# Moving the chunk loads and the copies within the stacks from SyncE's DMA queue to ScalarE's, with two more chunk buffers

## Chip, cores and metric

The kernel runs on one core of one Trainium2 chip. The metric is the device time of one execution in microseconds (us); three runs were timed, and one further execution was profiled.

## The reference

Three layers follow each other, on a batch of 2 with 768 positions:

```
attention: 8 heads of 64; q, k, v
  bits   = (q @ proj > 0), 6 bits, the same for k; bucket = the number that the bits spell
  scores = q @ k.T / 8, and -1e9 where the buckets of q and k differ
  x      = softmax(scores) @ v, heads side by side: 768 x 512 per batch
layer 1:  u = x + real(fft over positions and features of x)
  un = layernorm(u);  x = u + relu(un @ w_ch1) @ w_ch2        (w_ch1 512 x 2048, w_ch2 2048 x 512)
layer 2:  theta = x @ w_theta;  zr, zi = x cos(theta), x sin(theta)
  u = x + w_tok_r @ zr + w_tok_i @ zi;  out = u + relu(u @ w_ch)
```

The weights arrive as float64 and are handed to the kernel as pairs of 32-bit words; everything else is float32.

## The kernel before

**Order of the work.** Batch 0's attention comes first, in an order written out by hand (`attention_first`, every engine's instructions kept in the order of the source). After it, batch 0's FFT, layer norm and MLP run beside batch 1's attention (`attention`), then batch 1's FFT and MLP beside layer 2's theta, and the token sums last. Behind the first part the order on each engine is set by a planner: it lays the instructions out by a simulated timeline and by the priorities that `at(us)` gives (a smaller number goes first). FFT of batch 0 has 50, the conversion of w1 60 to 72 for its first 12 chunks and 51 to 54 for the last four, w2 100 to 115, attention of batch 1 from 115 with a pace of 2.6 per score tile (its loads and stacks 60 earlier), the MLP of batch 0 from 170. Each engine then works through its own list in order.

**Float64 chunks.** `from_f64` (L169) takes the next buffer of `cvs` in turn, loads one chunk of 128 x 512 float64 (512 KB) into it (tile `r`), rebuilds float32 from the two words with two ACTIVATEs on ScalarE and one shift-and-or on VectorE, in place. `conv16` (L183) then splits the chunk into two float16 parts: the high one by an ACTIVATE (into `w1h`, `w2h`), the low one by a subtraction on GpSimd (into `w1l`, `w2l`), which is the last to read the buffer. There are three buffers (`NCV`), and `T["c2"]` of a second pool, 0 here. 16 chunks are w1, 16 are w2, all converted between batch 0's attention and the middle of batch 1's. The chunks of w_theta, the token weights and w_ch come later, through the same function. All loads are issued by SyncE (`T["lc"] = 's'`).

**Gates.** `after_gate` wraps instructions in `tc.issue_after(m)`, which orders an instruction behind `m` only if both belong to the same engine, DMA issues counted to the engine that issues them. The first 12 chunks stand in `after_gate("cv")`, whose two members are the ScalarE copy and the VectorE subtraction of the last half tile that batch 0's attention turns on TensorE (`turn_half`, L368).

**Stacks.** For batch 1, `prep` (L271) loads q, k and v of a pair of heads (`tt`, `vr`) on SyncE and builds one stack (`stk`, L301) per head, the operands of the score matmuls: ScalarE rounds q into rows 0 and k into rows 2, a DMA copies each of the two to the other half of the partitions (192 KB, two per head, 16 in all), GpSimd writes the remainders, and ScalarE the bucket rows.

**Scores to values.** A score tile goes TensorE (`pss`), VectorE (row maximum `nm`), ScalarE (exponential `p`), a split into two float16 parts on ScalarE or GpSimd and GpSimd, a DMA transpose issued by SyncE (`transposed`, L379; into tiles that the trace shows as `pt<-p`, `pt<-pt`, `x<-p`), and TensorE again (`pso`). The layer norm's output for the MLP goes through SyncE's DMA transposes too (`unT<-u`). The MLP's first matmuls are `psm<-unT,w1h`.

Of the kernel before, what the change touches and what calls it, by code (L numbers as in the profile page):

```python
# [13 lines left out]
U32 = mybir.dt.uint32  # L14
# [19 lines left out]
def f(t):  # L34
    return t.bitcast(F32)
# [35 lines left out]
def fused_kernel(ctx, tc, A, out):  # L71
    nc = tc.nc
    V, AC, PE, PL, SY = (Ordered(tc, e) for e in (nc.vector, nc.scalar, nc.tensor, nc.gpsimd, nc.sync))

    def pool(name, bufs=1, **kw):
        return tc.alloc_tile_pool(name=name, bufs=bufs, **kw)

    def mk(p, shape, dt, tag, **kw):
        return p.tile(shape, dt, tag=tag, name=tag, **kw)

    def mm(o, l, r, st, sp):
        PE.matmul(o, l, r, start=st, stop=sp)

    def pl_copy(out, in_, scale=1.0):
        PL.tensor_scalar(out=out, in0=in_, scalar1=scale, scalar2=0.0, op0=ALU.mult, op1=ALU.add)

    def stt(eng, out, in0, in1, op, scale=1.0):
        if eng is V:
            return V.scalar_tensor_tensor(out=out, in0=in0, scalar=scale, in1=in1, op0=ALU.mult, op1=op)
        assert scale == 1.0  # L90
        return eng.tensor_tensor(out=out, in0=in0, in1=in1, op=op)

    T = dict(
        pet='dpd', dup=1, c2=0, c0=46, cx=0, wm=6, gf=1, o2=0, xs=1, sb=2, al=[['p', 2], ['p2', 3], ['pt', 3]], cs='v', g0=1,
        lg=[[0, 2], [2, 4], [4, 6]], ub=2, pace0=1.6, lead=60, f0=50.0, w1=60.0, w1s=1.0, b1=115, pace1=2.6,
        w2=100.0, w2s=1.0, m0=170.0, f1=190.0, th=240.0, m1=290.0, z0=330.0, wt=300.0, n0=8, n1=16, k0=12, k1=16, c1=46, tp=16, i0=40, i1=[20, 10],
        ne=42, es=150, ld='ss', lc='s', ps=[[0, 3], [0, 5], [1, 0], [1, 5]])
    P3 = ((0, 0), (0, 1), (1, 0))

    const = pool("const")  # L100
# [14 lines left out]
    def PS(k):  # L115
        n = turn[k] % sum(c for _, c in ring[k])
        turn[k] += 1
        for p, c in ring[k]:
            if n < c:
                w = [128, 2, 512] if k == "s" else [128, 512]  # L120
                tag = "psm" if p in [x[0] for x in ring["m"]] else "ps" + k
                live[k] = p.tile(w, F32, tag=tag, name=tag)
                return live[k]
            n -= c
# [27 lines left out]
    def fill(n, k="o"):  # L152

        for _ in range(n):
            PE.matmul(live[k][:, 392:512], pat[:, 0], pat[:, 1, 0:120], start=True, stop=True)
# [13 lines left out]
    def from_f64(src, scale=1.0, n=CN):  # L169
        p = cvs[turn["cv"] % len(cvs)]  # L170
        turn["cv"] += 1
        r = mk(p, [128, 2 * CN], U32, "r64", bufs=NCV if p is cv_p else None)
        r = r[:, 0:2 * n]
        {"s": SY, "a": AC, "p": PL}[T["lc"]].dma_start(out=r, in_=src.bitcast(U32))
        lo, hi = r[:, 0:2 * n:2], r[:, 1:2 * n:2]

        AC.activation(out=lo, in_=lo, func=AF.Relu, scale=2.0 ** -29 * (1 - 2.0 ** -20), bias=c_half)

        AC.activation(out=f(hi), in_=f(hi), func=AF.Prelu, scale=scale * 2.0 ** -112, alpha=2.0 ** 32)
        V.scalar_tensor_tensor(out=lo, in0=hi, scalar=3, in1=lo, op0=ALU.logical_shift_left, op1=ALU.bitwise_or)  # L180
        return f(lo)

    def conv16(src, n, hi, lo, lo_eng):  # L183
        for i in range(n // CN):
            c = slice(CN * i, CN * i + CN)
            w = from_f64(src[:, c], 2.0)
            AC.activation(out=hi[:, c], in_=w, func=AF.Copy)
            stt(lo_eng(i), lo[:, c], w, hi[:, c], ALU.subtract)
            yield

    def conv32(src, n, hi, lo):
        for i in range(n // CN):
            c = slice(CN * i, CN * i + CN)
            w = from_f64(src[:, c])
            AC.activation(out=hi[:, c], in_=w, func=AF.Copy)
            stt(PL, lo[:, c], w, f(hi[:, c]), ALU.subtract)
            yield
# [13 lines left out]
        "p": one(kept[0], 0, 1) + one(kept[2], 2) + one(spare[0], 4) + one(spare[1], 4),  # L211
        "p2": one(kept[1], 0, 1) + one(spare[0], 0, 1), "pt": one(kept[2], 0, 1) + one(spare[0], 2, 3) + one(spare[1], 0, 1, 2, 3)}
    cvs = [cv_p] * NCV
    if T["c2"]:
        cv2_p = pool("cv2", T["c2"], side="right")
        cvs += [cv2_p] * T["c2"]
# [54 lines left out]
    def prep(b, j):  # L271

        tt = mk(at_p, [128, 2, S], F32, "tt")
        ld = {"s": SY, "a": AC, "p": PL}[T["ld"][b]]
        vr = mk(at_p, [128, 2 * NT * (D + 1)], F32, "vr")
        for o, i in ((tt[:, 0], A["qT"]), (tt[:, 1], A["kT"]), (vr, A["v"])):
            ld.dma_start(out=o, in_=i[b, j])
        pl_copy(tt[:, 1], tt[:, 1], 0.125)
        v2 = mk(vv_p, [128, 2, 2 * NT * (D + 1)], F16, "vv")

        def values():
            AC.activation(out=v2[:, 0], in_=vr, func=AF.Copy, scale=VS)
            stt(V, v2[:, 1], vr, v2[:, 0], ALU.subtract, VS)

        if j:
            values()
        yield
        st = []
        bits = mk(at_p, [64, 2, 384], BF16, "bits")
        ps = PS("s")  # L290
        into = [ps[:, g, 0:384] for g in range(2)]
        for g in range(2):
            for qk in range(2):
                mm(into[g][32 * qk:32 * qk + 32], projb, tt[:, qk, 384 * g:384 * g + 384], True, True)
        V.tensor_scalar(out=bits, in0=ps[0:64, :, 0:384], scalar1=0.0, scalar2=None, op0=ALU.is_gt)
        made[4 * b + j] = [st, v2.rearrange("p a (h k c) -> p a h k c", h=2, k=NT)]
        for h in range(2):
            yield
            dd, oo = half[h], half[1 - h]
            s = mk(st_p, [128, 4, S], F32R, "stk")  # L300
            st.append(s)  # L301
            AC.activation(out=s[dd, 0], in_=tt[dd, 0], func=AF.Copy)
            SY.dma_start(out=f(s[dd, 1]), in_=f(s[dd, 0]))
            stt(PL, s[oo, 1], tt[dd, 0], f(s[dd, 0]), ALU.subtract)
            AC.activation(out=s[dd, 2], in_=tt[dd, 1], func=AF.Copy)
            SY.dma_start(out=f(s[oo, 3]), in_=f(s[dd, 2]))
            stt(PL, s[dd, 3], tt[dd, 1], f(s[dd, 2]), ALU.subtract)
            pp = PS("s")
            for g in range(2):
                mm(pp[:, g, 0:384], pat[0:64, h], bits[:, g], True, True)  # L310
            if b and not j and not h:
                fill(T["i0"])
            for qk in range(2):
                i = half[h if qk else 1 - h]
                AC.activation(out=s[oo, 2 * qk].rearrange("p (a n) -> p a n", a=2), in_=pp[i, :, 0:384],
                              func=AF.Sign if qk else AF.Relu, bias=hb[i, qk:qk + 1])
            if not j and not h:
                values()
        yield
# [96 lines left out]
    def attention(b, t0, pace, lead, hi_eng, lo_eng, after=lambda b, j: None):  # L416
        x_t[b] = mk(x_p, [128, NT, DM], F32, "x")
        n, w = 0, soft["p2"][0].shape[1]
        for j in range(4):
            i = 4 * b + j  # L420
            if i not in made:
                at(t0 + pace * n - lead)
                with after_gate("p1" if b else None):
                    run(prep(b, j))
# [503 lines left out]
    h1, l1, c1, c2 = (ev(k) for k in ("aapap", "p", "p", "p"))  # L928
# [8 lines left out]
    al = [x for t in kept for x in one(t, *range(t.shape[1]))]  # L937
# [33 lines left out]
    def mlp(b, t0, gs):  # L971
        for g in gs:
            timed(mlp1(b, g, m_p, res, hs), t0 + 41 * g, 2.6)
            timed(mlp2(b, g, hs), t0 + 41 * g + 20, 2.6)

    mlp(0, T["m0"], range(3))
    del cvs[NCV:]
    for p in ([cv2_p] if T["c2"] else []) + [so_p, sm_p, st_p, vv_p, at_p]:
        p.release()
    ring.pop("o")[0][0].release()  # L980
# [44 lines left out]
    def conv_tok(half, n0=0, n1=2 * NT):  # L1025
        for n in range(n0, n1):
            w = from_f64(A["wtok"][half][:, TH * n:TH * n + TH], n=TH)
            hi, lo = (wt(k, n % 2, n // 2) for k in range(2))
            AC.activation(out=hi, in_=w, func=AF.Copy)
            stt(PL, lo, w, f(hi), ALU.subtract)  # L1030
            yield
# [153 lines left out]
```

## Time and profile before

| | us |
|---|---|
| median of 3 timed runs | 730.92 |
| lowest and highest | 729.13, 737.44 |
| the profiled execution | 728.28 |
| its span, first to last instruction | 726.5 |
| TensorE busy | 664.8 |
| VectorE, ScalarE, GpSimd busy | 402.6, 372.7, 370.1 |

The profiled execution's own time is 1.8 us longer than its span. PE is TensorE (PEld its weight loads), DVE VectorE, ACT ScalarE, POOL GpSimd, SP SyncE; SPq is SyncE's instruction queue, where DMAs are issued and issues wait for semaphores. Because every operation is recorded in a helper, nearly all rows carry line L62 or L64; the tile names tell them apart. A wait is put down to the instruction that came last. Issuing a DMA is not counted as busy time.

### The profile page before, as it was taken

The page shows a single profiled execution, that of the slowest core. Times are in us where ns is not written, and L with a number is a line of the kernel's source. Part 1 is how long each engine was busy: PE and PEld are TensorE (multiplying, and loading weights), DVE is VectorE, ACT ScalarE, POOL GpSimd, SP SyncE. Part 2 cuts the span into 40 slices and gives each one's busy share as a digit, 9 for nine tenths or more (in the row PEclk, how much of TensorE's full clock was granted, in tenths as well). Part 3 has the DMA queues.
Part 4 walks back from the last instruction along what each step waited for, and adds up shares of the span by engine and source line. Part 5 has one row for each costly group of instructions (what it writes and reads, how often), then busy time and mean ns, then how long its engine had stood idle before and what let it go on. Part 6 is the DMA issues. An engine that isn't in the chain of part 4 may idle for free.

```text
span 726.5 us, 13450 instructions
## 1 busy us (share of the span) xinstructions
PE 664.8 (92%) x5424; PEld 510.9 (70%) x5424; DVE 402.6 (55%) x655; ACT 372.7 (51%) x597; POOL 370.1 (51%) x312
## 2 busy tenths in 40 slices
PE   5798988669668898999999999999999899999998
PEld 2365556557557655786686786687485599999997
DVE  1566787865999665543377583255422476751222
ACT  2565565766988898773423152065325676730010
POOL 3787789586878888776660020033403446930000
PEclk9999999978699999999999999999999999999999
DMA  9896967459889999776560043011004631720202
GB/s 327 186 187 141 157 121 142 93 164 213 197 206 240 269 231 253 151 145 124 102 195 27 13 120 65 1 45 30 1 1 145 223 89 39 234 81 25 88 1 87
DMA packets 161469, 93.68 MB, mean 129 GB/s; under 512 B 137088, under 2 KB 147584, under 8 KB 161408
## 3 DMA queue, kind: packets, MB, share of 16 engines
q1 hardware_dynamic: 159472, 86.27, 51.3%
q0 software_dynamic: 1936, 6.57, 2.6%
q8 instruction: 42, 0.69, 0.4%
q14 instruction: 19, 0.16, 0.1%
HBM read 49.82 MB, written 6.29 MB: 77 GB/s over the span
## 4 chain that ended last, share of the span: by engine, by line
PE 48%; POOL 10%; issue 9%; DMA 6%; ACT 5%; DVE 4%; POOLq 0%; SPq 0%; DVEq 0%; ACTq 0%
PE psm L62 31%; PE psf L62 14%; POOL p L62 3%; ACT r L62 2%; PE pso L62 2%; POOL w1l L62 2%; DMA x<-p 2%; POOL stk L62 2%; PE pss L62 1%; DMA r<-in_wtok 1%; DMA r<-in_w 1%; POOL pt L62 1%; DVE r L62 1%; ACT stk L62 1%; POOL w2l L62 1%
## 5 line engine op out<-in xcount | busy, mean ns | idle before, releaser
L62 PE MATMUL psm<-unT,w1h 128*128 128x256 f16 x768 | 130.4, 274 | 0.1
L62 PE MATMUL psm<-unT,w1l 128*128 128x256 f16 x384 | 105.2, 274 | 0.0
L62 DVE SCALAR_TENSOR_TENSOR r<-r 128x512 uint32<-128x512 uint32 (+1 forms) x64 | 64.6, 1016 | 51.9 <-ACT r L62 49.2
L62 PEld LDWEIGHTS <-w1h 128*128 128x128 f16 (+1 forms) x774 | 75.1, 99 | 15.5 <-issue 4.5
L62 PEld LDWEIGHTS <-hh 128*128 128x128 f16 x384 | 37.1, 98 | 42.8 <-issue 2.2
L62 POOL TENSOR_TENSOR w1l<-r,w1h 128x384 fp32r<-128x384 f32 (+1 forms) x36 | 41.9, 1178 | 43.5 <-ACT w1h L62 43.5
L62 PE MATMUL pss<-stk 128*128 128x384 f32 x192 | 48.8, 384 | 15.2 <-ACT p L62 9.4
L64 PE MATMUL pss<-stk 64*128 64x384 f32 (+1 forms) x288 | 55.4, 470 | 6.4 <-ACT p L64 3.2
L62 DVE TENSOR_REDUCE nm<-pss 128x1 f32<-128x768 f32 x48 | 44.9, 949 | 29.0 <-PE pss L62 28.8
L62 PE MATMUL psm<-w2h,hl 128*128 128x512 f16 x192 | 60.3, 379 | 0.0
L62 PE MATMUL psm<-w2l,hh 128*128 128x512 f16 x192 | 59.8, 379 | 0.2 <-POOL w2l L62 0.2
L62 ACT ACTIVATE r<-r,chalf 128x512 uint32<-128x512 uint32 (+1 forms) x64 | 46.1, 720 | 26.2 <-DMA r<-in_wtok 10.2
L62 PE MATMUL psm<-w2h,hh 128*128 128x512 f16 x192 | 59.3, 379 | 0.0
L62 POOL TENSOR_TENSOR p<-p,p 128x768 f16<-128x768 f32 x32 | 54.7, 1715 | 6.6 <-ACT p L62 5.5
L62 ACT ACTIVATE p<-pss,nm 128x768 f32<-128x768 f32 x48 | 42.5, 892 | 28.1 <-DVE nm L62 23.3
L62 DVE SCALAR_TENSOR_TENSOR hl<-psm,hh 128x512 f16<-128x512 f32 x48 | 32.8, 687 | 41.9 <-ACT hh L62 41.8
L64 DVE TENSOR_REDUCE nm<-pss 128x1 f32<-128x768 f32 x48 | 43.6, 950 | 19.9 <-PE pss L64 19.8
L62 ACT ACTIVATE hh<-psm 128x512 f16<-128x512 f32 x48 | 28.2, 590 | 40.4 <-PE psm L62 40.4
L62 PEld LDWEIGHTS pss<-stk 128*128 128x128 f32 x192 | 34.6, 204 | 20.2 <-ACT p L62 11.9
L62 PEld LDWEIGHTS <-w1l 128*128 128x128 f16 x384 | 37.7, 98 | 5.7 <-issue 1.2
L62 ACT ACTIVATE r<-r 128x512 f32<-128x512 f32 (+1 forms) x64 | 39.5, 618 | 0.0
L62 POOL TENSOR_TENSOR stk<-tt,stk 64x768 fp32r<-64x768 f32 x16 | 31.1, 1945 | 11.5 <-issue 9.6
(322 smaller groups left out, 1552.2 us busy)
## 6 DMA issues: line engine op xcount, KB each, us to landing
r<-in_w SPq DMA_DIRECT2D x32, 512.0 KB, 4.5
r<-in_wtok SPq DMA_DIRECT2D x24, 384.0 KB, 3.8
vr<-in_v SPq DMA_DIRECT2D x8, 390.0 KB, 3.6
stk<-stk SPq DMA_DIRECT2D x16, 192.0 KB, 3.8
xT<-xs SPq DMA_DIRECT2D x12, 256.0 KB, 2.6
xt<-xT SPq DMA_DIRECT2D x4, 768.0 KB, 5.8
ct<-in_ct POOLq DMA_DIRECT2D x4, 579.0 KB, 7.3
sn<-in_sn POOLq DMA_DIRECT2D x4, 576.0 KB, 8.2
```

The lines of the kernel that those rows point to most:

```text
L62: return fn(*a, **k)
L64: self.last = fn(*a, **k)
```

## The change

Five buffers take the place of three for the chunks of w1 and w2 (`c2` goes from 0 to 2), the loads into them go to ScalarE's DMA queue (`loads = [AC]`), and so do the 16 copies within the stacks. Behind batch 1's attention and batch 0's MLP in the source, the list `loads` is set to SyncE and the two extra buffers are dropped, so that the later chunks are loaded as before.

```diff
     T = dict(
-        pet='dpd', dup=1, c2=0, c0=46, ...
+        pet='dpd', dup=1, c2=2, c0=46, ...
...
-        ne=42, es=150, ld='ss', lc='s', ps=[[0, 3], [0, 5], [1, 0], [1, 5]])
+        ne=42, es=150, ld='ss', ps=[[0, 3], [0, 5], [1, 0], [1, 5]])
...
         r = r[:, 0:2 * n]
-        {"s": SY, "a": AC, "p": PL}[T["lc"]].dma_start(out=r, in_=src.bitcast(U32))
+        loads[0].dma_start(out=r, in_=src.bitcast(U32))
...
     cvs = [cv_p] * NCV
+    loads = [AC]
     if T["c2"]:
         cv2_p = pool("cv2", T["c2"], side="right")
         cvs += [cv2_p] * T["c2"]
...
             AC.activation(out=s[dd, 0], in_=tt[dd, 0], func=AF.Copy)
-            SY.dma_start(out=f(s[dd, 1]), in_=f(s[dd, 0]))
+            AC.dma_start(out=f(s[dd, 1]), in_=f(s[dd, 0]))
             stt(PL, s[oo, 1], tt[dd, 0], f(s[dd, 0]), ALU.subtract)
             AC.activation(out=s[dd, 2], in_=tt[dd, 1], func=AF.Copy)
-            SY.dma_start(out=f(s[oo, 3]), in_=f(s[dd, 2]))
+            AC.dma_start(out=f(s[oo, 3]), in_=f(s[dd, 2]))
...
     mlp(0, T["m0"], range(3))
     del cvs[NCV:]
+    loads[0] = SY
```

## Rows read from the trace of the kernel before

**Rows 1.** Busy time by stretch: PE, PEld, DVE, ACT, POOL; PEclk, DMA share, GB/s.
```profile
137.00:211.00 74.00, 52.56 (x427) 43.26 (x426) 58.59 (x111) 58.19 (x92) 57.82 (x43) 0.79 0.76 185
211.00:320.00 109.00, 99.83 (x1004) 73.98 (x1001) 72.14 (x93) 90.27 (x131) 91.46 (x63) 0.98 1.02 221
...
436.00:726.00 290.00, 284.72 (x1704) 236.90 (x1701) 117.52 (x175) 109.95 (x202) 79.69 (x76) 1.00 0.24 72
```

**Rows 2.** TensorE's waits, 137 to 211 us: us in total, times, longest.
```profile
PE pss L62 <- ACT p L62: 11.3, 6, 3.4
PE pss L62 <- ACT stk L62: 5.5, 3, 3.2
```

**Rows 3.** TensorE's waits, 211 to 320 us.
```profile
PE pso L62 <- DMA x<-p: 3.6, 3, 1.9
PE pso L62 <- DMA pt<-pt: 2.7, 3, 1.7
PE pso L62 <- DMA pt<-p: 2.2, 2, 1.9
```

**Rows 4.** ScalarE's waits for chunks, 137 to 211 us, then 126 to 320 us.
```profile
ACT r L62 <- DMA r<-in_w: 6.5, 4, 3.4
...
ACT r L62 <- DMA r<-in_w: 8.7, 9, 3.4
```

**Rows 5.** Waits of SyncE's queue, 137 to 211 us, then 211 to 320 us.
```profile
SPq L62 <- POOL w1l L62: 30.5, 14, 6.7
...
SPq L62 <- POOL w2l L62: 13.6, 10, 2.8
```

**Rows 6.** Issues by tile, r and stk: ns shortest/median/longest, first and last start.
```profile
L62 SPq DMA_DIRECT2D r<-in_w x32: 327/384/1377, 8.1 to 276.6; - x32
...
L62 SPq DMA_DIRECT2D stk<-stk x16: 461/472/953, 134.6 to 318.3; - x16
```

**Rows 7.** Timeline of SyncE's queue, the first loads: start, us.
```profile
8.08 1.40 SPq L62 DMA_DIRECT2D r<-in_w  x3
```

**Rows 8.** Timeline of ScalarE: last copy of a turned half, first conversion.
```profile
133.38 0.49 ACT L64 ACTIVATE w1l<-psm 128x384 f16<-128x384 f32 x1 [0.56 <-PE psm L64]
...
137.70 0.76 ACT L62 ACTIVATE r<-r,chalf 128x512 uint32<-128x512 uint32 x1
```

**Rows 9.** Groups of ScalarE's instructions, 137 to 211 us: busy, mean ns | idle before.
```profile
L62 ACT ACTIVATE r<-r,chalf 128x512 uint32<-128x512 uint32 x16 | 12.2, 763 | 6.6 <-DMA r<-in_w 6.5
```

**Rows 10.** Chain of waits, 137 to 215 us: start, us, what.
```profile
198.47 4.09 DMA r<-in_w
```

**Rows 11.** Timeline of SyncE's queue, 205 to 245 us.
```profile
221.45 0.52 SPq L62 DMA_DIRECT2D r<-in_w  x1
222.08 1.43 SPq L62 DMA_TRANSPOSE x<-p  x1
...
237.40 1.20 SPq L62 DMA_DIRECT2D stk<-stk  x2
238.70 0.54 SPq L62 DMA_DIRECT2D r<-in_w  x1
239.28 2.20 SPq L62 DMA_TRANSPOSE x<-p  x1
```

**Rows 12.** Timeline of GpSimd, 221 to 246 us.
```profile
230.40 1.65 POOL L62 TENSOR_TENSOR p<-p,p 128x768 f16<-128x768 f32 x1
```

**Rows 13.** Timeline of TensorE, 198 to 320 us; in brackets the idle time before.
```profile
210.93 0.38 PE L62 MATMUL psm<-unT,w1h 128*128 128x256 f16 x2
...
229.38 0.73 PE L62 MATMUL pso<-vv,x 128*128 128x65 f16 x18 [1.93 <-DMA x<-p]
...
246.72 0.55 PE L62 MATMUL pso<-vv,x 128*128 128x65 f16 x12 [1.14 <-DMA x<-p]
```

**Rows 14.** DMA issues, 126 to 320 us, then 320 to 370 us: median us to landing.
```profile
pt<-p SPq DMA_TRANSPOSE x12, 5.0
...
pt<-p SPq DMA_TRANSPOSE x4, 3.8
```

More of the change, by code (lines that the diff above doesn't have):

```diff
@@ L93, in fused_kernel @@
     T = dict(
-        pet='dpd', dup=1, c2=0, c0=46, cx=0, wm=6, gf=1, o2=0, xs=1, sb=2, al=[['p', 2], ['p2', 3], ['pt', 3]], cs='v', g0=1,
+        pet='dpd', dup=1, c2=2, c0=46, cx=0, wm=6, gf=1, o2=0, xs=1, sb=2, al=[['p', 2], ['p2', 3], ['pt', 3]], cs='v', g0=1,
         lg=[[0, 2], [2, 4], [4, 6]], ub=2, pace0=1.6, lead=60, f0=50.0, w1=60.0, w1s=1.0, b1=115, pace1=2.6,
         w2=100.0, w2s=1.0, m0=170.0, f1=190.0, th=240.0, m1=290.0, z0=330.0, wt=300.0, n0=8, n1=16, k0=12, k1=16, c1=46, tp=16, i0=40, i1=[20, 10],
-        ne=42, es=150, ld='ss', lc='s', ps=[[0, 3], [0, 5], [1, 0], [1, 5]])
+        ne=42, es=150, ld='ss', ps=[[0, 3], [0, 5], [1, 0], [1, 5]])
     P3 = ((0, 0), (0, 1), (1, 0))
```

## The prediction

> **What bounds the kernel now.** I read the busy time by stretches first [rows 1]. From 436 us to the end TensorE is busy 284.72 of 290 us: it alone sets that time, and the change touches nothing there. The moved instructions stand where batch 1's attention runs beside batch 0's FFT and MLP, and there TensorE is short of work. I call 137 to 211 us stage A (TensorE busy 52.56 of 74 us) and 211 to 320 us stage B (99.83 of 109). The end follows from TensorE's idle time before 320 us, so each edit counts by what it adds to or takes from the 21.4 us idle in A and the 9.2 in B. Then I read whom TensorE waits for. In A it is ScalarE, for the exponentials and the stacks: 11.3 and 5.5 us [rows 2]. In B it is the DMA transposes: 3.6, 2.7 and 2.2 us, 8.5 in sum [rows 3]. Last come the queues on both sides of the change. ScalarE waits for a chunk 6.5 us in A and 8.7 from 126 to 320 us, so 2.2 outside A [rows 4]. SyncE's queue stands on GpSimd's release of a chunk buffer, 30.5 us in 14 waits in A and 13.6 in 10 in B [rows 5]; transposes stand behind those waits.
>
> So the change takes work from a queue that hurts TensorE in B and gives it to an engine that TensorE waits for in A. ScalarE is busy 58.19 of 74 us in A and 90.27 of 109 in B [rows 1].
>
> **What moves, and when.** 32 loads of w1 and w2 and 16 copies within the stacks, 48 issues [rows 6]. Three loads go out together from 8.08 us now [rows 7], because the gate on the first twelve chunks orders only instructions of the gating instructions' own engines, and those are ScalarE and VectorE (the two copies of the last turned half). Once the loads are ScalarE's own instructions, the same gate holds them behind ScalarE's copy at 133.38 us [rows 8]. So the early loads are lost, not gained: five go out from about 134 us. The first chunk is converted at 137.7 us [rows 8], so batch 0's attention keeps its time; I put 0 to 126 us at no change (1.5 MB less in its first 20 us, beside tables that it does not read).
>
> **The cost on ScalarE.** The trace has no DMA issued by ScalarE. The nearest rows are SyncE's: a load issue 0.38 us, a copy issue 0.47 (medians) [rows 6]. The least is nothing, if the issue goes by while an ACTIVATE still runs; the most I take is the longest copy issue, 0.95, for one that first has to see ScalarE's own result land. I take the medians, the nearest rows. Sixteen chunks are converted in A [rows 9]; with five buffers 21 loads are issued by its end, and 8 of the copies, so A gets 21 x 0.38 + 8 x 0.47 = 11.8 us (0 to 27.6), and B gets 11 x 0.38 + 8 x 0.47 = 7.9 (0 to 18.1). Queued behind each of these on ScalarE are the exponentials that TensorE waits for.
>
> **What ScalarE gets back.** With five buffers a chunk lies ready before its conversion comes up, so I take the waits for chunks as gone: -6.5 us in A, -2.2 in B (0 to these). Against that the first conversion waits for a load issued after 134 us and landing some 4.1 us later [rows 10]; other ScalarE work can stand in between, and I put 1 us (0 to 3). Net on ScalarE: A 11.8 - 6.5 + 1 = +6.3, B 7.9 - 2.2 = +5.7.
>
> How much of this reaches TensorE? In A, ScalarE has 15.8 us idle, 9.3 without the waits for chunks, and these take up a part; but TensorE's waits in A are mostly for ScalarE. I take half: +3.2. In B the MLP fills TensorE, and its longest waits are the three of [rows 3], none for ScalarE; I take a quarter: +1.4. At the medians the two lie between -6.5 (waits gone, issues hidden) and +12 (both nets in full). At 0.95 us for every issue, with nothing absorbed and nothing won, it would be 27.6 + 18.1 + 3 = +48.7; that end is far from the nearest rows.
>
> **What SyncE's queue gives back.** Two copies and a load hold SyncE from 237.40 us, and only at 239.28 comes a transpose [rows 11] whose operand GpSimd had ready at 232.05 [rows 12]. TensorE waits 1.14 us for it [rows 13]: with the 1.88 us of moved work away, all of that goes. The transpose at 222.08 has one moved load ahead of it (0.63 us from 221.45), of a wait of 1.93. That is 1.1 + 0.6 = 1.7 us. The rest of these waits is the transposes of the layer norm, which stay on SyncE, and the landing. In A SyncE's waits for GpSimd stand mostly where no transpose is ready. I take -1.7, from 0 to -8.5.
>
> The landing itself: transposes take 5.0 us to land between 126 and 320 us and 3.8 once the loads are over [rows 14]. The DMA engines are full in B (share 1.02) [rows 1] and the same bytes still pass them, so I count no quicker landing. The Trainium skill says the same in "DMA: Bandwidth & Descriptors" (section "Issuing engines are not separate DMA queues"): DMAs issued by several engines run on the same 16 DMA engines, and only the sequencer's issue time is saved. Its section "Queues, rings and completion order" there speaks for a gain, since each DMA engine takes turns between the rows of the two issuers, packet by packet, so that a transpose would no longer stand behind a whole load; by it the landing could fall toward 3.8 us. No row here has two such queues at once.
>
> **Sum.** +3.2 + 1.4 - 1.7 = +2.9 us. The profiled execution is 728.28 us, its span 726.5 and 1.8 around it; it becomes 731.2. The median of the runs shown is 730.92, 2.6 above the profiled one, so I forecast 734 for the median. The order on every engine is planned anew with the change; that has no row, and I leave room for it in the range.
>
> **Rivals.**
> 1. Slower: ScalarE becomes the bound of A, because a refill stands at the head of its queue until GpSimd has released the buffer. The planner puts a load where the buffer is just released, so more buffers do not loosen that wait; what SyncE now stands through at little cost, ScalarE would stand through with the exponentials behind it. For it: SyncE's 30.5 us over 14 waits in A [rows 5], and ScalarE 79% busy there. Against: part of those waits is only SyncE having nothing else to do. Price: the net 6.3 plus a fifth of 30.5 (6.1), 12.4 us. It decides once ScalarE loses more in A than its 9.3 us of other idle time: from there the first MLP matmul, at 210.93 us now [rows 13], starts later by the whole. 730.92 + 12.4 = 743. Chance 0.34.
> 2. Faster: the queue was the trouble. Transposes go out when ready and land without loads ahead: three quarters of the 8.5 us in B (-6.4); and the load in the chain of waits shortly before the first MLP matmul (198.47 us, 4.09 long) is gone [rows 10], with ScalarE's issues hidden under running ACTIVATEs: -10.5. 720. For it: both waits are there in the rows. Against: ScalarE's share, and the full DMA engines. Chance 0.27.
> 3. It does little that counts: both sides come out small, 726 to 736. With the forecast this holds 0.39.
>
> **How the numbers follow.** A measurement of this kernel tells about 1% (7.3 us) from no change. Within 1%: 0.39; faster by more: 0.27 (rival 2); slower by more: 0.34 (rival 1). The likeliest case alone runs from 725 to 738. The range reaches from 719, past rival 2, to 747, past rival 1; the far end of +48.7 stays in the two in ten left out.
>
> **What would show it.** Right: no load of a chunk before 133 us, then five; ScalarE's waits for chunks under 2 us in A; TensorE's waits for transposes in B near 7 us; its waits for ScalarE in A near 20. Wrong towards slower: ScalarE's queue standing before loads with GpSimd's w1l as releaser, first MLP matmul after 218 us. Wrong towards faster: first MLP matmul before 206 us, transposes landing in under 4.2 us, TensorE idle in A under 16 us. The argument as a whole is wrong if the time changes by over 1% with these rows unchanged.

## The result and the profile after

The changed kernel takes 744.49 us (median of 20 executions, 732.43 to 753.26), the kernel before 730.83 us on the same chips (20, 725.55 to 737.44). The ratio is 1.0143, with a 95% interval of 1.0110 to 1.0176: 1.4% slower, some 10.5 us. The ratio, here and below, compares fast executions alone: eleven of the changed kernel's twenty, over 1.5% above its quickest, are left out of it as slow, and over all twenty the medians lie 1.9% apart. The profiled execution of the changed kernel happens to be the quickest of its twenty (732.43 us, span 730.7), so the profile of a second execution of the same kernel, `e1_again` (span 739.3), is read beside it.

Busy time by stretch, the changed kernel; columns as in [rows 1]:

```profile
137.00:211.00 74.00, 49.30 (x397) 41.35 (x394) 65.74 (x98) 61.59 (x101) 58.29 (x44) 0.82 0.92 218
211.00:320.00 109.00, 102.12 (x1009) 76.18 (x1008) 71.30 (x103) 82.35 (x118) 85.29 (x59) 1.00 0.93 195
320.00:436.00 116.00, 110.72 (x970) 82.06 (x969) 67.18 (x146) 44.70 (x73) 46.99 (x44) 0.99 0.50 105
```

The same of `e1_again`:

```profile
137.00:211.00 74.00, 47.78 (x378) 39.73 (x377) 61.55 (x86) 56.86 (x93) 54.83 (x41) 0.81 0.85 206
211.00:320.00 109.00, 99.48 (x979) 74.10 (x977) 66.53 (x106) 82.03 (x120) 82.74 (x57) 0.95 0.91 192
```

In stage A TensorE is idle 24.7 us (74 less 49.30) in the quick execution and 26.2 in the second, against 21.4 before [rows 1]. Behind stage B, from 320 to 436 us, it is idle 5.3 us in the changed kernel, where before it was busy nearly all the time:

```profile
320.00:436.00 116.00, 115.77 (x982) 86.03 (x980) 68.17 (x148) 42.58 (x72) 44.04 (x42) 1.00 0.43 99
```

`e7_new_order_one_queue`, below, has 4.9 us there, so this part comes with the new order of the work. Over the whole span TensorE is idle 69.9 us in the quick execution (730.7 less 660.8 busy) and 69.8 in the second (739.3 less 669.5), against 61.7 before (726.5 less 664.8). So in both it stands idle some 8 us longer. What sets the two apart is TensorE's busy time for the same matmuls, at a mean granted clock of 0.977 and 0.958.

Whom TensorE waits for in stage A, the changed kernel, answering to [rows 2]:

```profile
PE pso L62 <- DMA pt<-pt: 7.0, 2, 6.1
PE pso L62 <- DVE x L62: 5.2, 1, 5.2
PE pss L62 <- ACT p L62: 3.6, 2, 2.8
...
PE pss L62 <- ACT stk L62: 1.2, 1, 1.2
```

The waits for ScalarE, 16.8 us before, are 4.8. What stands in their place is two waits for transposes (7.0 us, one of them 6.1) and VectorE (which `e7_new_order_one_queue`, below, waits for as long, 4.9 us). This is not what a ScalarE burdened with 48 issues would look like. Its queue shows why. Issues by tile, answering to [rows 6]:

```profile
L62 ACTq DMA_DIRECT2D r<-in_w x32: 329/334/1285, 131.5 to 249.7; - x32
...
L62 ACTq DMA_DIRECT2D stk<-stk x16: 468/484/1702, 132.7 to 322.2; - x16
```

And ScalarE's timeline, its engine (ACT) and its queue (ACTq) together:

```profile
131.44 0.49 ACT L64 ACTIVATE w1l<-psm 128x384 f16<-128x384 f32 x1 [0.56 <-PE psm L64]
131.46 0.39 ACTq L62 DMA_DIRECT2D r<-in_w  x1
...
156.10 0.49 ACT L62 ACTIVATE fa<-psm 128x386 fp32r<-128x386 f32 x1 [1.70 <-PE psm L62]
156.16 0.33 ACTq L62 DMA_DIRECT2D r<-in_w  x1
```

An issue of 0.33 us begins 0.06 us after an ACTIVATE of 0.49 us and is over before it: the queue issues while the engine works. (The first load, at 131.46, stands right behind the last copy of a turned half, as the gate demands.)

What did get worse is how long transfers take to land. DMA issues from 126 to 320 us with the median us to landing, the changed kernel, then `e7_new_order_one_queue`, which has nearly the same order of work with all DMAs on SyncE:

```profile
stk<-stk ACTq DMA_DIRECT2D x14, 192.0 KB, 6.3
...
tt<-in_kT SPq DMA_DIRECT2D x3, 384.0 KB, 7.0
pt<-p SPq DMA_TRANSPOSE x11, 3.9
pt<-pt SPq DMA_TRANSPOSE x11, 5.5
```

```profile
stk<-stk SPq DMA_DIRECT2D x14, 192.0 KB, 3.5
...
tt<-in_kT SPq DMA_DIRECT2D x3, 384.0 KB, 4.2
pt<-p SPq DMA_TRANSPOSE x11, 4.4
pt<-pt SPq DMA_TRANSPOSE x11, 4.9
```

The copies within the stacks nearly double, 3.5 to 6.3 us, and a load that stayed on SyncE's queue (`tt<-in_kT`) takes 7.0 in place of 4.2; one kind of transpose is quicker, another slower. A median hides the few transfers that matter, as the experiments show.

The first MLP matmul, at 210.93 us before [rows 13], on TensorE's timeline of the changed kernel, then of `e1_again`:

```profile
212.07 0.38 PE L62 MATMUL psm<-unT,w1h 128*128 128x256 f16 x2
```

```profile
217.84 0.38 PE L62 MATMUL psm<-unT,w1h 128*128 128x256 f16 x2
```

### The profile page after: what moved, and what is told of

It reads as the page before. It is cut to its first block, busy times and chain, and to the rows that moved or that the text cites. A ratio compares the mean times of both kernels' runs of the same rounds, so it can differ in the third digit from the quotient of the medians.

```text
span 730.7 us, 13434 instructions
## 1 busy us (share of the span) xinstructions
PE 660.8 (90%) x5424; PEld 509.5 (70%) x5424; DVE 409.9 (56%) x655; ACT 372.8 (51%) x597; POOL 370.8 (51%) x312
## 4 chain that ended last, share of the span: by engine, by line
PE 45%; DMA 11%; issue 9%; POOL 6%; ACT 5%; DVE 1%; ACTq 1%; POOLq 0%; SPq 0%; DVEq 0%
PE psm L62 29%; PE psf L62 13%; DMA r<-in_w 3%; POOL p L62 2%; DMA x<-p 2%; DMA r<-in_wtok 2%; ACT r L62 2%; DMA pt<-pt 1%; ACT p L62 1%; PE pss L62 1%; PE pso L62 1%; DMA r<-in_wch 1%; POOL w2l L62 1%; POOL w1l L62 1%; POOL pt L62 1%
## 5 line engine op out<-in xcount | busy, mean ns | idle before, releaser
L62 DVE SCALAR_TENSOR_TENSOR r<-r 128x512 uint32<-128x512 uint32 (+1 forms) x64 | 69.4, 1095 | 44.4 <-ACT r L62 39.6
L62 POOL TENSOR_TENSOR w1l<-r,w1h 128x384 fp32r<-128x384 f32 (+1 forms) x36 | 43.5, 1222 | 42.7 <-ACT w1h L62 40.3
L62 PE MATMUL psm<-w2h,hh 128*128 128x512 f16 x192 | 61.1, 379 | 0.0
L64 PE MATMUL pss<-stk 64*128 64x384 f32 (+1 forms) x288 | 53.4, 457 | 6.9 <-ACT p L64 3.4
L64 DVE TENSOR_REDUCE nm<-pss 128x1 f32<-128x768 f32 x48 | 43.6, 950 | 18.2 <-PE pss L64 18.1
L62 PE MATMUL pso<-vv,pt 128*128 128x65 f16 x576 | 24.3, 198 | 18.2 <-DMA pt<-pt 10.8
```

Source lines behind the costliest of these rows:

```text
L62: return fn(*a, **k)
L64: self.last = fn(*a, **k)
```

## The experiments

**Parts of the change.** The first four kernels ran on one chip. `e1_again` is the changed kernel once more.

> The changed kernel once more, for a second profile: its profiled execution (732.4 us) was the quickest of twenty, whose median was 744.5. All theories: median 740 to 750. Queue theory (issues and waits on ScalarE's queue cost TensorE): TensorE waits for ScalarE over 15 us between 137 and 211 us. Buffer theory (with five buffers the conversions come in bursts, GpSimd runs without a pause and VectorE's merge of a chunk stands behind it): single merges of over 4 us, several of them, where the kernel before has one. Two-queue theory (chunks and transposes in the DMA engines at once): transposes land in over 5 us between 126 and 320 us and TensorE waits over 12 us for them.

It took 745.18 us, ratio 1.0125 (1.0068 to 1.0182): the loss is there again. TensorE waits 2.7 us for ScalarE in stage A, not over 15, which speaks against the queue theory as it is put there. It waits 13.4 us for transposes from 126 to 320 us, over the 12 of the two-queue theory, though of the three kinds of transposes only `pt<-pt` lands after more than 5 us (6.1).

`e2_buffers` has the two further buffers alone:

```diff
-        pet='dpd', dup=1, c2=0, c0=46, ...
+        pet='dpd', dup=1, c2=2, c0=46, ...
```

> Five buffers alone; loads and copies stay on SyncE. Queue theory: no loss, 728 to 733. Buffer theory: most of the loss is here, 739 to 745, with merges of over 4 us. Two-queue theory: no loss, 728 to 733. Plan theory (any new plan loses, since the settings were fitted to the old one): 734 to 745.

730.91 us, ratio 1.0043 (1.0018 to 1.0067). The buffers cost a little and gain nothing, though with them ScalarE waits less for chunks (4.6 us from 126 to 320 us, 8.7 before [rows 4]). The buffer theory, which puts most of the loss here, falls.

`e3_loads` moves the 32 loads alone, with three buffers; `e4_copies` the 16 copies alone:

```diff
-        {"s": SY, "a": AC, "p": PL}[T["lc"]].dma_start(out=r, in_=src.bitcast(U32))
+        loads[0].dma_start(out=r, in_=src.bitcast(U32))
```

```diff
-            SY.dma_start(out=f(s[dd, 1]), in_=f(s[dd, 0]))
+            AC.dma_start(out=f(s[dd, 1]), in_=f(s[dd, 0]))
...
-            SY.dma_start(out=f(s[oo, 3]), in_=f(s[dd, 2]))
+            AC.dma_start(out=f(s[oo, 3]), in_=f(s[dd, 2]))
```

> The chunk loads on ScalarE's queue alone, with three buffers; copies stay on SyncE. Queue theory: the larger part of the loss or more, since ScalarE now stands before the release of three buffers: 738 to 750, with ScalarE idle for GpSimd's w1l or w2l. Buffer theory: 728 to 733. Two-queue theory: 736 to 742. Plan theory: 734 to 745.

> The copies within the stacks on ScalarE's queue alone; three buffers, loads on SyncE. Queue theory: 16 issues of 0.5 us on ScalarE, 732 to 738. Buffer theory: 728 to 733. Two-queue theory: 730 to 735, since 3 MB are little. Plan theory: 734 to 745.

743.24 us, ratio 1.0201 (1.0172 to 1.0230), and 740.94 us, 1.0169 (1.0141 to 1.0198). Each part alone loses as much as the whole, so the loss is not a sum over issues. Sixteen issues of 0.5 us each, hidden under ACTIVATEs, cannot cost 12 us on ScalarE. But every one of these kernels also has an order of its own, since the planner, told of another queue, lays everything out anew. So the next four separate the order from the queue.

**Order or queue.** In these kernels the planner runs twice. The first time it plans one assignment of queues; the second time the instructions of each engine are tied to that order, and only the issues that change their queue are placed by the planner:

```diff
+    _, _, order = build(ORDER)          # plan for these queues
+    nc, arrays, _ = build(QUEUE, order) # issue on those, in that order
...
+            for n, e in order:
+                i = ins[n]
+                if str(i.engine) != e:
+                    continue
+                if e in last:
+                    tc.add_manual_dep(i, last[e].name, mybir.DependencyInfo(NoSync, DATA), reason="order")
+                last[e] = i
```

`e5_copies_old_order` has the copies on ScalarE in the order of before, `e8_loads_old_order` the loads, `e6_change_old_order` the whole change. `e7_new_order_one_queue` is the reverse: the order planned for the changed kernel, five buffers, everything issued by SyncE.

> Only the 16 copies are issued by ScalarE, and every engine keeps the order of the kernel before: the planner is run first for the kernel before, and its order on TensorE, VectorE, GpSimd, ScalarE and SyncE is laid on this one, into which the planner only sets the 16 issues on ScalarE. Plan theory (what costs is that the planner, told of another queue, lays the whole order out anew): the loss of e4_copies goes, within 0.5% of before (728 to 734 where before is 731). Queue theory (what costs is the second queue itself: issues on ScalarE, and transfers that reach the DMA engines together): the loss stays, 1 to 2% above before (738 to 745). A share of each: 0.5 to 1%.

> The whole change (five buffers, loads and copies on ScalarE's queue, first loads behind the last turned half at 131.5 us) under the order of the kernel before, except for the 48 issues. Plan theory: the loss of 1.2 to 1.4% goes, but for the 0.4% of the buffers and 1 to 3 us because the first chunks arrive at 136 us instead of lying ready: 0 to 0.8% above before (731 to 737), with the first MLP matmul near 211 us. Queue theory: 1.2 to 2% above before (740 to 746), landings of stack copies above 5 us and TensorE's waits for transposes up as in the changed kernel. A gain, below 728, would say that the queue helps and the new order alone loses.

> Five buffers, all DMAs on SyncE, but TensorE, VectorE, ScalarE's work and SyncE's other DMAs in the order that the planner lays out for the changed kernel; only the 48 issues are set among them, on SyncE. The first loads then start at 8 us again, since the gate holds ScalarE alone. Plan theory: the loss is in this order, 1 to 1.8% above before (738 to 744), with the first MLP matmul after 212 us. Queue theory: the loss goes with the queue, within 0.5% of before (728 to 735). If it is well above the changed kernel (over 1.5% above before), the second queue is worth something under the new order.

> Only the loads on ScalarE's queue, three buffers, under the order of the kernel before (e3_loads lost 2.0%). Plan theory: within 0.8% of before (730 to 737), the rest being the first chunks that arrive at 136 us and loads that stand on ScalarE in front of a release by GpSimd. Queue theory: 1.5 to 2.5% above before (742 to 749), as in e3_loads.

| kernel | us | ratio | 95% interval |
|---|---|---|---|
| e5: copies on ScalarE, order of before | 737.73 | 1.0123 | 1.0077 to 1.0169 |
| e6: whole change, order of before | 742.19 | 1.0163 | 1.0088 to 1.0237 |
| e7: order of the changed kernel, one queue | 730.23 | 1.0031 | 1.0002 to 1.0060 |
| e8: loads on ScalarE, order of before | 743.40 | 1.0189 | 1.0118 to 1.0259 |

The plan theory falls on all four. The new order with the five buffers costs 0.3% on one queue; the second queue costs 1.2 to 1.9% under the old order. Of the change's 1.43%, about 1.1 are the queue's, some 8 us. These 8 us count all that the second queue brings, the later first loads included.

Since e5 has the order of the kernel before on all engines, its time can be followed DMA by DMA. It runs level with before until a transpose issued at 238 us. Timeline of e5: SyncE's queue, ScalarE's queue, and the matmul that needs the transpose:

```profile
237.88 0.33 SPq L62 DMA_DIRECT2D r<-in_w  x1
238.30 3.57 SPq L62 DMA_TRANSPOSE x<-p  x1
...
238.73 0.50 ACTq L62 DMA_DIRECT2D stk<-stk  x1
239.26 0.61 ACTq L62 DMA_DIRECT2D stk<-stk  x1
...
250.36 0.84 PE L62 MATMUL pso<-vv,x 128*128 128x65 f16 x12 [4.68 <-DMA x<-p]
```

Before, the two copies and the load stood ahead of this transpose, it was issued at 239.28 [rows 11], and the matmul began at 246.72 after a wait of 1.14 us [rows 13]. Now it is issued 0.98 us earlier, and the matmul begins 3.64 us later. The same happens at 271 us (8.4 us to landing, 6.8 before), and most plainly at 320, where the chunk loads are over: a transpose goes out at 320.55 and two copies on ScalarE's queue at 320.54 and 321.27. DMA view of e5, 320 to 328 us (busy tenths of the 16 DMA engines and GB/s, each in 40 slices of 0.2 us, then issues with us to landing):

```profile
DMA  9999800079999839999999999959911913690030
GB/s 212 223 212 198 175 10 0 0 169 215 230 138 123 111 60 223 242 224 232 204 155 172 165 183 125 116 73 93 106 22 35 134 28 54 125 141 8 0 108 0
...
stk<-stk ACTq DMA_DIRECT2D x2, 192.0 KB, 5.6
pt<-p SPq DMA_TRANSPOSE x1, 9.1
```

The same transpose and copies before, 316 to 322 us:

```profile
stk<-stk SPq DMA_DIRECT2D x2, 192.0 KB, 3.0
pt<-p SPq DMA_TRANSPOSE x1, 3.9
```

9.1 us in place of 3.9. The reader should look at the five slices from 324.8 us (9, 9, 5, 9, 9 tenths): they move 73 to 125 GB/s, where the five from 323 us, most of them the transpose alone, move over 200 at the same busy share. The transfers do not only wait for each other, they get slower.

e8 shows it with loads in ScalarE's queue. DMA view, 213 to 230 us (slices of 0.425 us), and the matmul that waits:

```profile
DMA  8971097899199999209999979137799799999999
GB/s 279 376 318 39 0 200 159 157 200 139 15 163 49 26 38 60 8 10 203 157 54 87 67 48 103 42 143 145 236 214 176 164 275 270 224 210 173 321 334 217
...
pt<-p SPq DMA_TRANSPOSE x1, 13.8
```

```profile
228.57 1.17 PE L62 MATMUL pso<-vv,pt 128*128 128x65 f16 x18 [9.17 <-DMA pt<-p]
```

A load on one queue, and copies with a transpose on the other: in the four slices from 218.1 us the engines are 90% busy or more at 26 to 60 GB/s, the transpose lands after 13.8 us, and TensorE waits 9.17 us. But e8's loss is not all of this kind. The gate holds its first three loads until 133 us, and beside them the stacks' first four copies, which stayed on SyncE's queue, land after 7.4 us (the median from 126 to 150 us), 2.8 before. TensorE waits 8.4 us for the stacks, 5.5 before, and the first MLP matmul stands at 216.43 us, 5.5 later than before, ahead of the collision shown.

**Which copies.** If the loss is made where a transpose meets copies of the other queue, the copies that meet none should be free. In e5's trace copies 1 to 4 go out with no transpose on its way, and 5, 6, 13 and 14 beside one that was issued over 2.5 us earlier and lands 1.3 us later at most. The other eight go out within 1.1 us of a transpose's issue.

```diff
-            SY.dma_start(out=f(s[dd, 1]), in_=f(s[dd, 0]))
+            (AC if next(Q["n"]) in Q["copies"] else SY).dma_start(out=f(s[dd, 1]), in_=f(s[dd, 0]))
```

> e5_copies_old_order with only eight of the 16 copies on ScalarE's queue: number 1 to 6, 13 and 14, those that there met no transpose of SyncE's queue or took no harm from it; the other eight are issued by SyncE again, every engine in the order of the kernel before. Collision theory (a DMA transpose of one queue and copies of another that run together hold each other up; all else on the second queue is free): within 0.3% of before (about 728 where before is 728). Price-per-issue theory (each DMA that ScalarE issues costs the same, 9.3 us over 16): 0.5 to 0.7% above (732 to 733).

> The other half: copies 7 to 12, 15 and 16 on ScalarE's queue, among them the six that in e5_copies_old_order landed 7 to 11 us after their issue beside a transpose that took 8 to 12. Collision theory: the whole loss, 0.9 to 1.4% above before (735 to 738). Price-per-issue theory: 0.5 to 0.7% (732 to 733), as with the first half.

e9: 727.95 us, ratio 0.9988 (0.9964 to 1.0013). e10: 740.32 us, 1.0164 (1.0122 to 1.0206). Eight copies on ScalarE's queue cost nothing, and the other eight cost as much as all sixteen did (the intervals overlap; a little above the 0.9 to 1.4% that I expected). One price for every issue is out. TensorE's timeline at the same matmul, e9, then e10:

```profile
246.46 0.55 PE L62 MATMUL pso<-vv,x 128*128 128x65 f16 x12 [1.13 <-DMA x<-p]
```

```profile
249.96 0.84 PE L62 MATMUL pso<-vv,x 128*128 128x65 f16 x12 [4.78 <-DMA x<-p]
```

Six of the eight free copies go out before stage B, so an issue that costs ScalarE something in B alone would give nearly the same two times. TensorE's waits speak against it. From 126 to 340 us, in us, those for transposes (`pt<-pt`, `pt<-p`, `x<-p`) and those for ScalarE (`p`, `stk`), and its idle time over the whole span:

| kernel | for transposes | for ScalarE | idle |
|---|---|---|---|
| before | 10.2 | 17.2 | 61.7 |
| e9: eight copies apart | 7.7 | 18.9 | 62.2 |
| e5: all copies | 16.3 | 16.1 | 66.9 |
| e10: eight copies that meet | 18.0 | 14.2 | 66.5 |
| e7: new order, one queue | 6.7 | 5.9 | 63.7 |
| the changed kernel | 14.5 | 4.8 | 69.9 |
| e6: whole change, order of before | 19.0 | 17.8 | 69.2 |
| e8: loads, order of before | 17.9 | 18.2 | 71.1 |

Against the kernel with the same order, the waits for transposes grow by 6 to 9 us wherever the second queue costs time, in the changed kernel against e7 too (7.8). Those for ScalarE grow by 1 us at most, e9 aside, which loses nothing.

Idle time is not all of it. e5's span is 9.5 us longer than before; 5.2 of them are idle, and 4.3 are TensorE's busy time (669.1 against 664.8) for the same matmuls. After its long wait the twelve matmuls of e5's timeline take 0.84 us in place of 0.55. Busy time and granted clock around them (columns as in [rows 1]), e5, then before:

```profile
248.10:254.90 6.80, 4.54 (x44) 3.26 (x45) 0.69 (x1) 4.32 (x6) 3.70 (x4) 0.50 1.16 285
```

```profile
248.20:251.60 3.40, 3.40 (x34) 2.85 (x33) 0.63 (x1) 3.34 (x5) 3.30 (x3) 0.50 1.15 280
```

A clock of 0.50 is TensorE's lower level, 1.2 of 2.4 GHz. In e5 it begins here within the wait of 4.68 us, and there are three more stretches of 3.4 us at it, from 217.3, 282.2 and 330.0 us, each right behind a wait for a transpose. Before, the one shown is the only one from 211 to 340 us. So a late transpose costs TensorE its wait and, in these traces, a slower stretch behind it.

**The transfers by themselves.** Both kernels leave out the attention and all other computation; they hold transfers alone, a few one-column operations of VectorE between the groups and, in part of the second, work to fill the engines.

```diff
+    cases = [
+        [(turn, SY)], [(copy, SY)], [(copy, AC)], [(load, SY)], [(load, AC)],
+        [(turn, SY), (copy, SY)], [(turn, SY), (copy, AC)],
+        [(turn, SY), (load, SY)], [(turn, SY), (load, AC)],
+        [(copy, SY), (load, SY)], [(copy, SY), (load, AC)],
+    ]
```

> The transfers by themselves: the attention and everything else are left out, and after each group a few one-column operations of VectorE wait for all of its transfers, so that the groups stand alone, five of each kind: a transpose as pt<-p; two copies as stk<-stk; a 512 KB load; and pairs of these on one queue or on SyncE's and ScalarE's. Collision theory: alone, each lands in 2.5 to 4.5 us on either queue; transpose and copies on one queue, 3.5 to 6; on two queues, 7 to 12 us for both; copies and a load on two queues no longer than on one (4 to 6). Whether a transpose and a load collide like that, the theory leaves open: 8 us or more if the transpose is what matters, under 7 if it is the copy within SBUF. If the second queue slows whatever it meets, copies and a load on two queues take over 7 us too. If it is none of this but the crowd of other transfers, all pairs land within 6.

DMA view of `e11_pairs`: a transpose and two copies, five times on one queue (111 to 142 us), then on two (142 to 178); a queue's line gives packets, MB and its packets' time as a share of 16 engines, q1 being SyncE's queue and q10 ScalarE's:

```profile
q1 hardware_dynamic: 8640, 3.93, 64.0%
...
stk<-stk SPq DMA_DIRECT2D x10, 192.0 KB, 3.2
pt<-p SPq DMA_TRANSPOSE x5, 3.7
...
q1 hardware_dynamic: 7840, 1.97, 40.9%
q10 hardware_dynamic: 800, 1.97, 25.6%
...
stk<-stk ACTq DMA_DIRECT2D x10, 192.0 KB, 5.3
pt<-p SPq DMA_TRANSPOSE x5, 5.9
```

The same view for two copies and a load, on one queue (242 to 271 us), then on two (271 to 302):

```profile
q1 hardware_dynamic: 1520, 4.59, 56.3%
...
q10 hardware_dynamic: 720, 2.62, 27.2%
q1 hardware_dynamic: 799, 1.97, 25.6%
```

The times of the 8,640 packets of transposes and copies add up to 0.640 x 31 us x 16 = 317 us on one queue and 0.665 x 36 x 16 = 383 on two: 21% more for the same bytes. The copies' packets have 147 us of the 383 (0.256 x 36 x 16), about what they take alone (141, from 42.7% of 46.4 to 67 us), so nearly all of the increase is in the transposes' packets. Packet times can overlap (the share in [rows 1] is 1.02), so their sum can be more than the time for which the engines are held. But the five groups also take longer as a whole, 36 us in place of 31.

Copies and loads add up to 0.563 x 29 x 16 = 261 and 0.528 x 31 x 16 = 262, nothing more, though the five groups take 31 us in place of 29, the copies land after 3.8 us in place of 2.7 and the load after 4.8 in place of 3.9. A transpose and a load add up to 317 us on one queue and 324 on two, 2% more, and the five groups take 31 us in place of 33. The transpose lands after 5.4 us in place of 3.7 and the load after 4.1 in place of 4.4, which is no more than sharing the engines. So the large increase needs a transpose and copies within SBUF. On landing, my expectation was too high: 5.9 us and 5.3, not 7 to 12. Alone, copies land after 2.7 us from either queue.

The last run asks what makes it 8 to 12 in the kernels.

```diff
+    cases = [
+        [(turn, SY), (turn2, SY), (copy, SY)], [(turn, SY), (turn2, SY), (copy, AC)],
+        [(load, SY), (turn, SY), (copy, SY)], [(load, SY), (turn, SY), (copy, AC)],
+        [(turn, SY), (copy, SY), (busy, None)], [(turn, SY), (copy, AC), (busy, None)],
...
```

> Again transfers by themselves, attention and all else left out, five of each group. It asks why a transpose that meets two copies of the other queue took 8 to 12 us in the kernels and 5.5 to 6.6 us in e11_pairs. Crowd theory: what stands ahead on SyncE's queue does it, as at 320 us (another transpose) and at 238 us (a load) of e5_copies_old_order. Then two transposes, or a load and a transpose, with the copies on the other queue, have a transpose that lands 8 us or more after its issue, against 5 to 6.5 with everything on SyncE's queue. Surroundings theory: the engines' own traffic to SBUF does it. Then one transpose and two copies on two queues, beside full-width work of ScalarE, VectorE and GpSimd, take 8 us or more, and those without it stay under 7. If neither, all stay under 7, and the size of a collision in the kernels is left open.

DMA view of `e12_crowd`: a load, a transpose and two copies, on one queue (90 to 129.5 us), then the copies on the other (129.9 to 182):

```profile
q1 hardware_dynamic: 9360, 6.56, 70.8%
...
pt<-p SPq DMA_TRANSPOSE x5, 5.0
...
q1 hardware_dynamic: 8560, 4.59, 49.1%
q10 hardware_dynamic: 800, 1.97, 19.6%
...
pt<-p SPq DMA_TRANSPOSE x5, 9.2
```

With a load ahead of it the transpose lands after 9.2 us, as in the kernels, the packets' times add up to 28% more (0.687 x 52.1 x 16 = 573 us against 0.708 x 39.5 x 16 = 447), and the five groups take 52.1 us in place of 39.5. Work on ScalarE, VectorE and GpSimd adds nothing: the plain pair beside it takes 5.9 us again, so the surroundings theory falls. The crowd theory holds by half, for two transposes with the copies on the other queue land after 6.2 us, not 8.

## Why the prediction was right and wrong

The time lies inside the range of 719 to 747 us, 10 us above the forecast of 734, and slower by more than 1%, to which I had given 0.34. It came near rival 1's 743, but not by rival 1's mechanism. That it lies in the range is luck: the upper end was set by a rival that did not happen, and the sum had nothing for what did.

- **The gate and the early loads: right.** The first load is issued at 131.46 us and five are out by 139; the first conversion waits 0.64 us for its chunk, and 0 to 126 us keeps its TensorE time, 103.26 against 103.92 us. What the step left out is that the loads now run beside the stacks' first copies. From 126 to 150 us these land after 8.0 us (median), 2.8 before, and TensorE waits 1.6 us for one.
- **ScalarE's price, 11.8 us in A and 7.9 in B: wrong, nearly all of it.** I took the medians of SyncE's issues as time that ScalarE loses; the right value was near the lower bound, which I had named ("if the issue goes by while an ACTIVATE still runs"): in the changed kernel's chain of waits from 137 to 215 us ScalarE's queue has 2.5%, some 2 us. In the order of before with the copies moved (e5), TensorE's waits for ScalarE from 126 to 340 us are 16.1 us (10.5 for p and 5.6 for stk) against 17.2, and e9's eight copies cost nothing. That the changed kernel shows only 4.8 us of them in A goes with its new order: e7, with no issue on ScalarE, has 5.9 from 126 to 320 us. My mark, "its waits for ScalarE in A near 20", failed.
- **The waits for chunks: wrong.** ScalarE still waits 4.6 us for them in A (6.5 in `e1_again`), not under 2, and the two buffers by themselves cost 0.4%.
- **SyncE's relief, -1.7 us: the step happened and its result turned over.** In e5 the transpose at 238 us does go out 0.98 us earlier. It lands 3.6 us later. My mark for stage B, waits for transposes near 7 us, held roughly (5.4 us, 8.0 in `e1_again`), but 9.1 us of them now stand in A (5.4 in `e1_again`), 1.7 before.
- **"I count no quicker landing": the step that failed.** I argued from full DMA engines and unchanged bytes that landing would not get better, and did not ask whether it could get worse. It does where a transpose of one queue meets copies of the other. I had set this term at 0; under nearly one order (e7 and the changed kernel) TensorE's waits for transposes are 6.7 and 14.5 us. The second queue as a whole costs about 8 us (1.43% less e7's 0.31%), the longer stretches at the lower clock among them: my sum counted TensorE's idle time alone, and in e5 4.3 of 9.5 us are busy time. The DMA rows of before could not show it, as they hold one queue; but then its size was unknown on both sides, and it ought to have had a bound on the side of loss.
- **The new plan, left to the range: 0.3%**, order and buffers together (e7).
- **Rival 1** needed ScalarE's queue standing on GpSimd's release. In the changed kernel ScalarE's waits from 126 to 320 us name GpSimd's release for 0.6 us alone, and e5, which moves no load, loses 1.2%. **Rival 2** wanted TensorE to wait less for transposes; from 126 to 340 us it waits 14.5 us for them in place of 10.2. I gave the slower side one mechanism, and it was another.

The two sections of the Trainium skill's page "DMA: Bandwidth & Descriptors" can be set beside this now. "Issuing engines are not separate DMA queues" says that DMAs of several engines share the same 16 DMA engines and that issuing from several saves only issue time. The trace agrees in that no run here gained from the second queue (e9, the nearest, has a ratio of 0.9988 with 1 in its interval), and copies and loads have 261 us of packet time on one queue and 262 on two. With transposes and copies more than issue time changed: 383 us against 317. "Queues, rings and completion order" says that each DMA engine takes turns between the rows, packet by packet. I drew from it that a transpose would no longer stand behind a load. The other side of taking turns counted too: a transpose that was issued first shares the engines with the copies behind it and lands after 5.9 us in place of 3.7. Taking turns leaves open why the five groups take longer as a whole, 36 us in place of 31.

What stays open: why a transpose's packets take longer when a copy's packets of another queue run beside them, and why a load ahead of the transpose makes it worse (9.2 us) when another transpose does not (6.2). Loads on ScalarE's queue beside transposes and copies on SyncE's, as in e8, were not tried by themselves, so how the moved loads' loss divides between collisions and the later first loads is not shown. Transposes on ScalarE's queue together with the copies were not tried. Nor was the loss of the changed kernel traced collision by collision, as e5's was at its main ones.

## What to carry to other kernels

Before moving DMAs to a second queue, look at what the first keeps: copies within SBUF that go out beside a DMA transpose belong in that transpose's queue, where they wait their turn. Eight copies that met no transpose, or only the end of one, moved for nothing, and their issues cost nothing on a ScalarE that was working. For loads from HBM the runs show a loss in the kernels, but not this cause by itself. To tell a queue's cost from that of a new plan, tie the instructions to the old order and move the issues alone. And where an edit puts something into the profile that it has never shown, such as two queues at once, bound that term on the side of loss as well.

## What the runs showed of the hardware

- ScalarE's queue issues DMAs while the engine computes: 0.33 us for a load beside a running ACTIVATE of 0.49 us; a copy's issue takes 0.48 (median).
- With a transpose and copies within SBUF on two queues the packets' times add up to 21% more than on one, 28% with a load ahead; with copies and a load to nothing more, with a transpose and a load to 2%. The increase is in the transpose's packets. In e8 engines that were over 90% busy moved as little as 26 GB/s in a slice.
- The issue itself stretches: the transpose at 238.30 us of e5 held SyncE's queue 3.57 us, 2.20 before [rows 11].
- With a wait of 4.68 us for a transpose TensorE's granted clock was 0.50 for 6.8 us (e5), with one of 1.14 us, before, for 3.4.
